# Attention decode with a gated FFN, forward and backward: the FFN's work cut into chains and put into another order

## The chip, the cores and the metric

The kernel runs on one core of a Trainium2 chip. The metric is the time of one execution on the device in microseconds. A core has five engines with a queue each: PE (TensorE, matrix products), DVE (VectorE), ACT (ScalarE), POOL (GpSimd) and SP (SyncE); in this kernel SP starts the loads and POOL the stores. Every engine takes its instructions in the order in which the build has put them.

## The reference, cut to what matters

One token attends to a cache of 4096 keys and values in 32 heads of 128, and beside it runs a gated FFN of width 1376. Wanted are the output and the gradients of x, of both caches and of all weights.

```python
xn  = layernorm(x)                                  # 1 x 512
q   = xn @ wq                                       # 32 heads x 128
p   = softmax((q @ k.T) * 128**-0.5)                # 1 x 4096 in each head
out = x + (p @ v) @ wo + (gelu(xn @ w_gate) * (xn @ w_up)) @ w_down
# and the gradients of sum(out * grad_out): dx, dk, dv, dwq, dwo, dw_gate, dw_up, dw_down
```

For one token dv of a head is the outer product of p and of the head's share of `grad_out @ wo.T`; dk is that of q and the gradient of the scores; every weight gradient is an outer product too. So large arrays are read once (K and V, 1 MB each in each head) and arrays as large are written once (dK and dV).

The FFN needs: g and u (the two products with xn), gelu and its derivative `dgl`, h = gelu(g)·u, `f = h @ w_down`, `dh = grad_out @ w_down.T`, then dg and du from dh (together `dgu`), dw_gate and dw_up as outer products of xn with dg and du, dw_down as that of h and grad_out, and the share of dx, `dg @ w_gate.T + du @ w_up.T`. The two products with a transposed weight need the weight blocks transposed on PE first.

## The kernel before, in words

Each head passes three stages, written as Python generators. `stage1(h)` (L133) loads K and V, 1 MB each, into a ring of six buffers (three heads), transposes each in 32 blocks of 128x128 on PE (L126), eight blocks to a PSUM tile, and copies each tile back: three on ScalarE (L130), the fourth on VectorE (L128). `stage2(h)` (L177) makes the scores in 32 narrow matmuls (L183), the softmax as a chain of small steps (L186 to L201: the maximum over partitions through a matmul with the identity, exp, the sum through a matmul with ones), dP with the transposed V (L205), and the gradient of the scores DS (L209 to L216). `stage3(h)` (L235) makes O (L247) and DQ (L266) from the untransposed V and K; these two free the buffers for a later head's load. It makes dV (L258) and dK (L272) on VectorE, 2.3 us each, and stores each by POOL (L263, L277); dV and dK share two buffers, so dV of a head waits until dV of the head before has been written. For every four heads dwo (L282) and dwq (L308) are stored.

Iteration h of the main loop (L573) lets `stage3(h)`, `stage2(h+1)` and `stage1(h+2)` take turns. The FFN is a further generator, `ffn_gen` (L319). Its first step, after iteration GATE_LOAD_H = 23, loads the three weights (4.2 MB) by POOL. To hold that load back, one element of each weight tile is first written by VectorE from `gate_t`, which head 23's O has filled. The later steps run after iterations 29, 30 and 31, nine at a time, and begin with `xn_g`, a copy of xn that is gated by head 29's O. What is left runs after the loop.

The order of the generators is not yet the order on the engines. The framework (Tile) schedules: it takes the program's order as a priority and its own estimate of when operands are ready, and puts each engine's instructions into one fixed queue. So an operation can stand far from where the code has it.

The FFN's steps before: the loads; g and u (L342, 88 narrow matmuls) and their roundings; gelu and its derivative (L354 to L384); f (L390, 44 matmuls) and dw_down (`dwd`, L397, in groups of four blocks, two buffers); eleven blocks of w_down transposed (L413), copied by ScalarE (L416) and multiplied with grad_out to dh (L421); dgu (L426 to L436); its transpose `tpr` (L439) and the broadcast of dg and du to all partitions (L450 on PE, L454 on ScalarE); the eight stores of dw_gate and dw_up (`dwt`, L459 and L460, two buffers); and eight times: transpose one 128-row strip of w_gate or w_up (L469, L473: 11 blocks), copy it by ScalarE (L470, L474), multiply it with dg or du (L478). After the loop the closing sums (L587 to L609) make the two small outputs.

PSUM: the narrow products, `gu_ps`, `f_ps`, `dh_ps`, `dx_ps`, the broadcasts and each head's scores (`SDP`) share three buffers of the tag `sdp`; all transposes share three of the tag `tp`.

Of the kernel before, what the change touches and what calls it, by code (L numbers as in the profile page):

```python
# [31 lines left out]
GATE_H = 29  # L32
GATE_LOAD_H = 23
# [14 lines left out]
def kernel(  # L48
# [268 lines left out]
    def ffn_gen():  # L317
        fsb1 = ffn_pools["fsb1"]
        fsb3 = ffn_pools["fsb3"]  # L319
        if True:  # L320
# [3 lines left out]
            gate0 = gate_t[:, 1:2]  # L324
            for wt in (wg_sb[:, 0, 0:1], wu_sb[:, 0, 0:1], wd_sb[:, 0, 0:1]):
                nc.vector.tensor_scalar(out=wt, in0=ones_bf[:, 0:1], scalar1=gate0, scalar2=None, op0=ALU.bypass)
            nc.gpsimd.memset(wg_sb[:, :, F:FPAD], 0.0)
            nc.gpsimd.memset(wu_sb[:, :, F:FPAD], 0.0)
            nc.gpsimd.memset(wd_sb[96:128, FT - 1, :], 0.0)
            nc.gpsimd.dma_start(out=wg_sb[:, :, 0:F], in_=B_w_gate.rearrange("(c p) f -> p c f", p=P))  # L330
            nc.gpsimd.dma_start(out=wu_sb[:, :, 0:F], in_=B_w_up.rearrange("(c p) f -> p c f", p=P))
            nc.gpsimd.dma_start(out=wd_sb[:, 0:FT - 1, :], in_=B_w_down[0:(FT - 1) * P, :].rearrange("(ft p) j -> p ft j", p=P))
            nc.gpsimd.dma_start(out=wd_sb[0:96, FT - 1, :], in_=B_w_down[(FT - 1) * P:F, :])
# [3 lines left out]
            gu_ps = lps.tile([P, 512], FP32, tag="sdp")  # L337
            for which, w_sb in enumerate((wg_sb, wu_sb)):
                for ft in range(FT):
                    col = which * 16 + ft  # L340
                    for c in range(NC):
                        nc.tensor.matmul(gu_ps[:, col:col + 1], lhsT=w_sb[:, c, ft * P:(ft + 1) * P], rhs=xn_g[:, c:c + 1],  # L342
                                         start=(c == 0), stop=(c == NC - 1))
            g_bf = fsb1.tile([P, FT], BF16)
            u_bf = fsb1.tile([P, FT], BF16)
            nc.vector.tensor_copy(out=g_bf[:], in_=gu_ps[:, 0:FT])
            nc.vector.tensor_copy(out=u_bf[:], in_=gu_ps[:, 16:16 + FT])
            g = fsb1.tile([P, FT], FP32)
            u = fsb1.tile([P, FT], FP32)
            nc.vector.tensor_copy(out=g[:], in_=g_bf[:])  # L350
            nc.vector.tensor_copy(out=u[:], in_=u_bf[:])
            yield
            g2 = fsb1.tile([P, FT], FP32)
            nc.vector.tensor_tensor(out=g2[:], in0=g[:], in1=g[:], op=ALU.mult)  # L354
            poly = fsb1.tile([P, FT], FP32)
            nc.vector.tensor_scalar(out=poly[:], in0=g2[:], scalar1=GELU_A, scalar2=1.0, op0=ALU.mult, op1=ALU.add)
            inner = fsb1.tile([P, FT], FP32)
            nc.vector.tensor_tensor(out=inner[:], in0=poly[:], in1=g[:], op=ALU.mult)
            th = fsb1.tile([P, FT], FP32)
            nc.scalar.activation(out=th[:], in_=inner[:], func=ACT.Tanh, scale=GELU_C)  # L360
            cdf = fsb1.tile([P, FT], FP32)
            nc.vector.tensor_scalar(out=cdf[:], in0=th[:], scalar1=0.5, scalar2=0.5, op0=ALU.mult, op1=ALU.add)
            gelu = fsb1.tile([P, FT], FP32)
            nc.vector.tensor_tensor(out=gelu[:], in0=cdf[:], in1=g[:], op=ALU.mult)
            gelu_bf = fsb1.tile([P, FT], BF16)
            nc.vector.tensor_copy(out=gelu_bf[:], in_=gelu[:])
            gelu_r = fsb1.tile([P, FT], FP32)
            nc.vector.tensor_copy(out=gelu_r[:], in_=gelu_bf[:])
            h_f = fsb1.tile([P, FT], FP32)
            nc.vector.tensor_tensor(out=h_f[:], in0=gelu_r[:], in1=u[:], op=ALU.mult)  # L370
            h_bf = fsb1.tile([P, FT], BF16)
            nc.vector.tensor_copy(out=h_bf[:], in_=h_f[:])
            h_r = fsb1.tile([P, FT], FP32)
            nc.vector.tensor_copy(out=h_r[:], in_=h_bf[:])
            t2 = fsb1.tile([P, FT], FP32)
            nc.vector.tensor_tensor(out=t2[:], in0=th[:], in1=th[:], op=ALU.mult)
            omt2 = fsb1.tile([P, FT], FP32)
            nc.vector.tensor_scalar(out=omt2[:], in0=t2[:], scalar1=-0.5 * GELU_C, scalar2=0.5 * GELU_C, op0=ALU.mult, op1=ALU.add)
            poly3 = fsb1.tile([P, FT], FP32)
            nc.vector.tensor_scalar(out=poly3[:], in0=g2[:], scalar1=3.0 * GELU_A, scalar2=1.0, op0=ALU.mult, op1=ALU.add)  # L380
            dgl = fsb1.tile([P, FT], FP32)
            nc.vector.tensor_tensor(out=dgl[:], in0=omt2[:], in1=poly3[:], op=ALU.mult)
            nc.vector.tensor_tensor(out=dgl[:], in0=dgl[:], in1=g[:], op=ALU.mult)
            nc.vector.tensor_tensor(out=dgl[:], in0=dgl[:], in1=cdf[:], op=ALU.add)  # L384
            yield
            f_ps = lps.tile([P, 512], FP32, tag="sdp")
            for c in range(NC):
                for ft in range(FT):
                    fs = min(P, F - ft * P)
                    nc.tensor.matmul(f_ps[:, c:c + 1], lhsT=wd_sb[0:fs, ft, c * P:(c + 1) * P], rhs=h_bf[0:fs, ft:ft + 1],  # L390
                                     start=(ft == 0), stop=(ft == FT - 1))
            nc.vector.tensor_copy(out=ffn_col[:], in_=f_ps[:, 0:NC])
            for ft in range(FT):
                fs = min(P, F - ft * P)
                if ft % 4 == 0:
                    dwd4 = fsb3.tile([P, 4, D_MODEL], BF16, tag="dwd4")
                nc.vector.tensor_scalar(out=dwd4[0:fs, ft % 4, :], in0=dy_bcast[0:fs, :], scalar1=h_r[0:fs, ft:ft + 1], scalar2=None, op0=ALU.mult)  # L397
                if ft % 4 == 3:
                    nc.gpsimd.dma_start(out=out_8[(ft - 3) * P:(ft + 1) * P, :].rearrange("(e p) j -> p e j", p=P), in_=dwd4[:])
                elif ft == FT - 1:  # L400
                    n_full = ft % 4
                    f0 = (ft - ft % 4) * P
                    if n_full > 0:
                        nc.gpsimd.dma_start(out=out_8[f0:f0 + n_full * P, :].rearrange("(e p) j -> p e j", p=P), in_=dwd4[:, 0:n_full, :])
                    nc.gpsimd.dma_start(out=out_8[ft * P:F, :], in_=dwd4[0:fs, ft % 4, :])
            yield
            dh = fsb1.tile([P, FT], FP32)
            nc.vector.memset(dh[96:128, FT - 1:FT], 0.0)
            for ft in range(FT):
                fs = min(P, F - ft * P)  # L410
                tpd = lps_t.tile([P, 8 * P], BF16, tag="tp")
                for c in range(NC):
                    nc.tensor.transpose(out=tpd[:, c * P:c * P + fs], in_=wd_sb[0:fs, ft, c * P:(c + 1) * P], identity=ident_bf[0:fs, 0:fs])  # L413
                wdT = fsb3.tile([P, NC, P], BF16, tag="wdT")
                if fs == P:
# [224 lines left out]
```

## Time and profile before

| what | value |
|---|---|
| time, median of six runs | 496.13 us (492.22 to 499.04) |
| the profiled execution's own time | 498.88 us |
| its span, first to last instruction | 496.7 us |
| PE busy, weight loads busy | 387.3 us (78%), 359.5 us (72%) |
| VectorE busy | 319.8 us (64%) |
| ScalarE busy | 261.1 us (53%) |
| GpSimd busy | 59.0 us (12%) |
| moved by DMA | 164.73 MB, mean 332 GB/s |
| mean granted TensorE clock | 0.643 |

How to read it: the span is the profiled execution's, and what lies around it (2.2 us) is in its time but not in the trace. The second part of the page cuts the span into 40 slices of 12.4 us; each digit is a busy share in tenths, and a row under them gives the GB/s that the transfers moved. A timeline row has start, duration, engine, line, operation, the tile written and the tiles read; in square brackets the idle time of that engine before it and what ended it. L numbers are lines of the kernel before.

### The profile page before, as it was taken

The page shows a single profiled execution, that of the slowest core. Times are in us where ns is not written, and L with a number is a line of the kernel's source. Part 1 is how long each engine was busy: PE and PEld are TensorE (multiplying, and loading weights), DVE is VectorE, ACT ScalarE, POOL GpSimd, SP SyncE. Part 2 cuts the span into 40 slices and gives each one's busy share as a digit, 9 for nine tenths or more (in the row PEclk, how much of TensorE's full clock was granted, in tenths as well). Part 3 has the DMA queues.
Part 4 walks back from the last instruction along what each step waited for, and adds up shares of the span by engine and source line. Part 5 has one row for each costly group of instructions (what it writes and reads, how often), then busy time and mean ns, then how long its engine had stood idle before and what let it go on. Part 6 is the DMA issues. An engine that isn't in the chain of part 4 may idle for free.

```text
span 496.7 us, 16676 instructions
## 1 busy us (share of the span) xinstructions
PE 387.3 (78%) x7309; PEld 359.5 (72%) x7309; DVE 319.8 (64%) x1067; ACT 261.1 (53%) x414; POOL 59.0 (12%) x107
## 2 busy tenths in 40 slices
PE   3588838697779788987898878985998699775691
PEld 3578727687678777977888877984898598674591
DVE  3156863687577767777566746784775266788364
ACT  1367806375456554663556546573456466532571
POOL 0100001010011001101110001100130002012122
PEclk9968956578557855686556555595557555775555
DMA  7977999599999999999997999989899979966547
GB/s 285 389 286 255 357 381 377 189 343 335 392 337 370 337 385 369 370 379 343 361 350 307 316 368 351 382 317 384 317 381 384 420 285 347 402 243 252 189 158 269
DMA packets 44509, 164.73 MB, mean 332 GB/s; under 512 B 19666, under 2 KB 23764, under 8 KB 27540
## 3 DMA queue, kind: packets, MB, share of 16 engines
q1 hardware_dynamic: 30924, 79.70, 46.5%
q0 software_dynamic: 13504, 83.96, 41.8%
q8 instruction: 57, 0.93, 0.7%
q14 instruction: 16, 0.13, 0.1%
q10 hardware_dynamic: 8, 0.00, 0.0%
HBM read 83.92 MB, written 79.73 MB: 329 GB/s over the span
## 4 chain that ended last, share of the span: by engine, by line
issue 63%; DMA 10%; PE 9%; POOL 8%; DVE 7%; ACT 1%; SPq 0%; POOLq 0%; ACTq 0%; DVEq 0%
PE tp L126 4%; DMA out_dram<-dK_sb 4%; POOL out_dram L263 3%; POOL out_dram L277 2%; DMA wo_1277<-in_A_wo_dram 2%; DMA K_sb<-in_A_k_cache_dram 2%; DVE dK_sb L272 2%; DVE dV_sb L258 1%; DMA out_dram<-dV_sb 1%; POOL out_dram L282 1%; POOL out_dram L308 1%; PE DQ_ps L266 1%; PE SDP L183 1%; DMA out_dram<-dwt 1%; DVE junkw L152 1%
## 5 line engine op out<-in xcount | busy, mean ns | idle before, releaser
L130 ACT COPY KT_sb<-tp 128x1024 bf16<-128x1024 bf16 x96 | 93.6, 1016 | 84.0 <-PE tp L126 77.2
L126 PE MATMUL tp<-ident_bf,K_sb 128*128 128x128 bf16 x1024 | 109.0, 282 | 18.8 <-DMA K_sb<-in_A_k_cache_dram 11.7
L126 PE MATMUL tp<-ident_bf,V_sb 128*128 128x128 bf16 x1024 | 108.6, 281 | 14.6 <-ACT VT_sb L130 8.7
L130 ACT COPY VT_sb<-tp 128x1024 bf16<-128x1024 bf16 x96 | 93.4, 1017 | 28.0 <-PE tp L126 25.3
L126 PEld LDWEIGHTS <-V_sb 128*128 128x128 bf16 x1024 | 91.4, 129 | 22.6 <-issue 20.6
L126 PEld LDWEIGHTS <-K_sb 128*128 128x128 bf16 x1024 | 90.4, 129 | 21.3 <-DMA K_sb<-in_A_k_cache_dram 12.7
L263 POOL DMA_DIRECT2D out_dram<-dV_sb x32 | 17.2, 538 | 216.7 <-DVE hilo L170 79.9
L266 PEld LDWEIGHTS <-K_sb 128*128 128x128 bf16 x1024 | 32.5, 103 | 12.4 <-issue 12.3
L183 PE MATMUL SDP<-Q_bf,KT_sb 128*128 128x1 bf16 x1024 | 38.2, 166 | 2.1 <-DVE hilo L170 1.8
L266 PE MATMUL DQ_ps<-DS_bf,K_sb 128*128 128x1 bf16 x1024 | 32.8, 166 | 8.3 <-DVE DS_bf L216 8.2
L183 PEld LDWEIGHTS <-KT_sb 128*128 128x128 bf16 x1024 | 36.3, 104 | 3.0 <-DVE KT_sb L128 1.9
L205 PEld LDWEIGHTS <-VT_sb 128*128 128x128 bf16 x1024 | 31.4, 102 | 7.8 <-issue 7.5
L162 ACT COPY wqTh<-tpw 128x512 bf16<-128x512 bf16 x32 | 18.9, 590 | 33.1 <-PE tpw L160 33.1
L205 PE MATMUL SDP<-DO_bf,VT_sb 128*128 128x1 bf16 x1024 | 32.2, 165 | 4.5 <-DVE tot L174 4.4
L247 PE MATMUL O_ps<-P_bf,V_sb 128*128 128x1 bf16 x1024 | 33.5, 166 | 0.7 <-DVE P_bf L201 0.7
L247 PEld LDWEIGHTS <-V_sb 128*128 128x128 bf16 x1024 | 32.9, 103 | 0.8 <-issue 0.7
L277 POOL DMA_DIRECT2D out_dram<-dK_sb x32 | 17.2, 539 | 131.4 <-DVE dxq_acc L290 26.8
L128 DVE COPY VT_sb<-tp 128x1024 bf16<-128x1024 bf16 x32 | 21.9, 685 | 10.7 <-PE tp L126 9.8
L128 DVE COPY KT_sb<-tp 128x1024 bf16<-128x1024 bf16 x32 | 21.9, 685 | 8.0 <-PE tp L126 7.3
L174 DVE TENSOR_SCALAR tot<-SDP 128x1 f32<-128x1 f32 x64 | 13.8, 218 | 20.0 <-PE SDP L172 19.8
L160 PE MATMUL tpw<-ident_bf,wqh 128*128 128x128 bf16 x128 | 18.1, 276 | 6.7 <-DVE KT_sb L128 6.0
L270 ACT ACTIVATE DSexp<-DS_f 128x64 bf16<-128x64 f32 x32 | 8.3, 260 | 23.4 <-DVE DS_f L213 23.4
(316 smaller groups left out, 604.8 us busy)
## 6 DMA issues: line engine op xcount, KB each, us to landing
K_sb<-in_A_k_cache_dram SPq DMA_DIRECT2D x32, 1024.0 KB, 8.3
V_sb<-in_A_v_cache_dram SPq DMA_DIRECT2D x32, 1024.0 KB, 9.5
out_dram<-dV_sb POOLq DMA_DIRECT2D x32, 1024.0 KB, 8.6
out_dram<-dK_sb POOLq DMA_DIRECT2D x32, 1024.0 KB, 8.2
wq_chunk<-in_A_wq_dram SPq DMA_DIRECT2D x4, 1024.0 KB, 7.3
wqh<-in_A_wq_dram SPq DMA_DIRECT2D x32, 128.0 KB, 10.9
out_dram<-dwo_sb POOLq DMA_DIRECT2D x8, 512.0 KB, 8.6
out_dram<-dwt POOLq DMA_DIRECT2D x8, 344.0 KB, 3.2
```

The costliest lines, as they stand in the source:

```text
L126: nc.tensor.transpose(out=tp[:, t8 * P:(t8 + 1) * P], in_=src[:, t, :], identity=ident_bf[:, :])
L128: nc.vector.tensor_copy(out=dstT[:, g4 * 8:(g4 + 1) * 8, :], in_=tp[:, :])
L130: nc.scalar.copy(out=dstT[:, g4 * 8:(g4 + 1) * 8, :], in_=tp[:, :])
L160: nc.tensor.transpose(out=tpw[:, c * P:(c + 1) * P], in_=wqh[:, c, :], identity=ident_bf[:, :])
L162: nc.scalar.copy(out=wqTh[:], in_=tpw[:, 0:NC * P].rearrange("p (c i) -> p c i", c=NC))
L174: nc.vector.tensor_scalar(out=tot[:], in0=SDP[:, c0:c0 + 1], scalar1=SDP[:, c0 + 1:c0 + 2], scalar2=None, op0=ALU.add)
L183: nc.tensor.matmul(SDP[:, C_S + t:C_S + t + 1], lhsT=KT_sb[:, t, :], rhs=Q_bf[:, h:h + 1], start=True, stop=True)
L205: nc.tensor.matmul(SDP[:, C_DP + t:C_DP + t + 1], lhsT=VT_sb[:, t, :], rhs=DO_bf[:, h:h + 1], start=True, stop=True)
L247: nc.tensor.matmul(O_ps[:, h:h + 1], lhsT=V_sb[:, t, :], rhs=P_bf[:, t:t + 1], start=(t == 0), stop=(t == T - 1))
L263: nc.gpsimd.dma_start(out=out_3[0, h].rearrange("(p t) d -> p t d", p=P), in_=dV_sb[:])
L266: nc.tensor.matmul(DQ_ps[:, h:h + 1], lhsT=K_sb[:, t, :], rhs=DS_bf[:, t:t + 1], start=(t == 0), stop=(t == T - 1))
L277: nc.gpsimd.dma_start(out=out_2[0, h].rearrange("(p t) d -> p t d", p=P), in_=dK_sb[:])
```

## The change: the FFN as interleaved chains

The FFN begins one head earlier (GATE_H 28, GATE_LOAD_H 22), and takes seven steps instead of nine after each iteration from there on. w_down is loaded ahead of the other two weights. The code of the FFN is moved into functions: `chainA(ft)`, one block of dh with its transposes; `chainB1` to `chainB3`, g and u, gelu, and f with dw_down; `chainC(c, which)`, the transposes of one strip of w_gate or w_up; `chainF(c, which)`, the product with that strip. They are called alternately. `dh` multiplies with `dy_g`, a copy of grad_out that is gated as `xn_g` is. The strips have a buffer each (eight instead of two in turn), since four are transposed before dgu is there. `dwd4` has one buffer instead of two. The stores of dw_gate and dw_up come after all strips.

```diff
-GATE_H = 29
-GATE_LOAD_H = 23
+GATE_H = 28
+GATE_LOAD_H = 22
...
+            nc.gpsimd.dma_start(out=wd_sb[:, 0:FT - 1, :], in_=B_w_down[0:(FT - 1) * P, :].rearrange("(ft p) j -> p ft j", p=P))
+            nc.gpsimd.dma_start(out=wd_sb[0:96, FT - 1, :], in_=B_w_down[(FT - 1) * P:F, :])
             nc.gpsimd.dma_start(out=wg_sb[:, :, 0:F], in_=B_w_gate.rearrange("(c p) f -> p c f", p=P))
             nc.gpsimd.dma_start(out=wu_sb[:, :, 0:F], in_=B_w_up.rearrange("(c p) f -> p c f", p=P))
-            nc.gpsimd.dma_start(out=wd_sb[:, 0:FT - 1, :], in_=B_w_down[0:(FT - 1) * P, :].rearrange("(ft p) j -> p ft j", p=P))
-            nc.gpsimd.dma_start(out=wd_sb[0:96, FT - 1, :], in_=B_w_down[(FT - 1) * P:F, :])
...
+            dy_g = fsb1.tile([P, NC], BF16)
+            nc.vector.tensor_scalar(out=dy_g[:], in0=dy_col_bf[:], scalar1=gate_t[:, 0:1], scalar2=None, op0=ALU.bypass)
...
-                    nc.tensor.matmul(dh_ps[0:fs, 0:1], lhsT=wdT[:, c, 0:fs], rhs=dy_col_bf[:, c:c + 1], start=(c == 0), stop=(c == NC - 1))
+                    nc.tensor.matmul(dh_ps[0:fs, 0:1], lhsT=wdT[:, c, 0:fs], rhs=dy_g[:, c:c + 1], start=(c == 0), stop=(c == NC - 1))
...
+            def chainC(c, which):
+                w_sb = wg_sb if which == 0 else wu_sb
+                wT = fsb1.tile([P, FT, P], BF16, tag=f"wT{c}{which}")
+                tpa = lps_t.tile([P, 8 * P], BF16, tag="tp")
+                for ft in range(8):
+                    nc.tensor.transpose(out=tpa[:, ft * P:(ft + 1) * P], in_=w_sb[:, c, ft * P:(ft + 1) * P], identity=ident_bf[:, :])
+                nc.scalar.copy(out=wT[:, 0:8, :], in_=tpa[:, :].rearrange("p (k i) -> p k i", k=8))
...
+                        dwd4 = fsb3.tile([P, 4, D_MODEL], BF16, tag="dwd4", bufs=1)
...
+            corder = [(c, w) for c in range(NC) for w in range(2)]
+            g, u = chainB1()
+            yield
+            chainA(0); chainA(1); yield
+            gelu_r, h_bf, h_r, dgl = chainB2(g, u)
+            yield
+            chainA(2); chainA(3); yield
+            chainC(*corder[0]); yield
+            chainA(4); chainA(5); yield
+            chainB3(h_bf, h_r); yield
+            chainC(*corder[1]); yield
+            chainA(6); chainA(7); yield
+            chainC(*corder[2]); yield
+            chainA(8); chainA(9); yield
+            chainC(*corder[3]); yield
+            chainA(10)
             dh_bf = fsb1.tile([P, FT], BF16)
...
+            def chainF(c, which):
+                wT = wTs[(c, which)]
+                dx_ps = lps.tile([P, 512], FP32, tag="sdp")
+                for ft in range(FT):
+                    col = which * FT + ft
+                    nc.tensor.matmul(dx_ps[:, 0:1], lhsT=wT[:, ft, :], rhs=dgu_bf[:, col:col + 1], start=(ft == 0), stop=(ft == FT - 1))
+                nc.vector.tensor_copy(out=dxn8[:, 2 * c + which:2 * c + which + 1], in_=dx_ps[:, 0:1])
...
+            for k in range(4):
+                chainF(*corder[k])
+            yield
...
+            for k in range(4, 8):
+                chainC(*corder[k])
+                chainF(*corder[k])
+                yield
+            nc.vector.tensor_reduce(out=dxn_ffn[:], in_=dxn8[:, :].rearrange("p (c w) -> p c w", w=2), axis=AXX, op=ALU.add)
             for which, (src_b, out_ap) in enumerate(((dg_bcast, out_6), (du_bcast, out_7))):
...
-            for _ in range(9):
+            for _ in range(7):
```

## The prediction

> **What bounds the kernel now.** I read the transfer rows first, then the timeline from 400 us on, then the transfers.
>
> ```profile
> DMA  7977999599999999999997999989899979966547
> GB/s 285 389 286 255 357 381 377 189 343 335 392 337 370 337 385 369 370 379 343 361 350 307 316 368 351 382 317 384 317 381 384 420 285 347 402 243 252 189 158 269
> ```
>
> For most of the span the 16 DMA engines are nine tenths busy or more; the change moves no byte out of it. From slice 36 on (435 us) 158 to 269 GB/s are left, so instruction chains set the end there. Busy time by stretch (columns: stretch and length, then busy us of PE, its weight loads, VectorE, ScalarE, GpSimd, then clock, DMA share, GB/s):
>
> ```profile
> 430.00:440.00 10.00, 8.95 (x139) 8.03 (x139) 7.30 (x20) 6.63 (x11) 0.74 (x2) 0.71 0.69 282
> 440.00:450.00 10.00, 6.50 (x234) 6.28 (x233) 8.72 (x39) 0.98 (x4) 1.39 (x3) 0.63 0.59 234
> 450.00:460.00 10.00, 5.09 (x103) 4.82 (x104) 8.51 (x29) 3.91 (x8) 2.64 (x4) 0.50 0.76 290
> 460.00:470.00 10.00, 7.50 (x88) 5.49 (x88) 3.88 (x17) 4.76 (x9) 2.35 (x4) 0.50 0.55 209
> 470.00:480.00 10.00, 9.10 (x204) 8.84 (x204) 5.09 (x27) 6.57 (x12) 1.98 (x4) 0.50 0.33 120
> ```
>
> VectorE carries 430 to 460; 460 to 480 is a chain through PE with VectorE half idle. The timeline's landmarks (start, us, engine, line):
>
> ```profile
> 428.33 0.34 PE L183 MATMUL SDP<-Q_bf,KT_sb 128*128 128x1 bf16 x8
> ...
> 445.90 2.29 DVE L272 TENSOR_TENSOR dK_sb<-b_8577,DSexp 128x4096 bf16<-128x4096 bf16 x1
> ...
> 456.39 2.27 DVE L272 TENSOR_TENSOR dK_sb<-b_8577,DSexp 128x4096 bf16<-128x4096 bf16 x1
> ...
> 463.12 0.28 PE L439 MATMUL tpr<-ident_bf,dgu_bf 128*22 128x128 bf16 x1 [1.85 <-DVE dgu_bf L435]
> ...
> 468.56 1.04 PE L183 MATMUL SDP<-Q_bf,KT_sb 128*128 128x1 bf16 x32
> ...
> 478.82 0.16 DVE L267 CAST DQ_bf<-DQ_ps 128x1 bf16<-128x1 f32 x1 [1.56 <-PE DQ_ps L266]
> ...
> 481.43 2.29 DVE L258 TENSOR_TENSOR dV_sb<-b_8588,Pexp 128x4096 bf16<-128x4096 bf16 x1
> ...
> 484.90 0.59 DVE L459 TENSOR_SCALAR dwt<-du_bcast,xn_colf 128x1408 bf16<-128x1408 bf16 x1 [0.69 <-DMA out_dram<-dwt]
> ```
>
> In order: head 30's scores end (428.7); head 29's dK (445.9); head 30's dK (456.4); the FFN gradient `dgu` reaches PE (463.1); head 31's scores (468.6); its DQ is copied out (478.8); its dV (481.4); the last `dwt` waits for its buffer (484.9). So head 30's softmax runs *beside* the K and V loads of head 31, and only head 31's stands in the open tail.
>
> **The change, step by step.** The arithmetic stays: the same transposes, matmuls and copies, plus one 128x4 gate copy (`dy_g`, 0.22 us by its twin at L336). What changes is the order, so I read the order in which the built kernel puts its instructions on each engine, and walked those queues, each in order, with the durations above.
>
> *Weights one head earlier.* wg, wu and wd (4.2 MB) go onto POOL's queue one head sooner. The transfers are saturated there (388 and 394 GB/s between 360 and 400 us), so this trades places: zero, bounds -3 to +3 us (0.69 to 1.02 DMA share in the rows from 400 to 440). It holds head 27's dV at about 421 us, as before (421.9): that waits for the write of head 26's dV.
>
> *Up to head 29's dK: +4.3 us.* On VectorE dV and dK of 27 now stand ahead of the last copy of V 29's transposes, and head 29's `negb` behind dV of 28. With 8.6 us as the median landing of a dV, dV 28 starts at 431.5, `negb` at 433.9; exp, VT 30's copy (0.68) and dK 28 follow to 437.6. Then P of 29 at 439 (its sum's matmul stands behind 16 wd and 11 wg transposes on PE), DS 443, dV 29 444.1 to 446.4. Ahead of dK 29 now stand the `dh` copies of chains A4 and A5, behind K 31's 29 transposes on PE (about 0.127 us each, L469's eight in 1.01): dK 29 starts at 450.2, not 445.9. Bounds: -4 (VectorE never waits) to +8 (both dV waits a full landing longer).
>
> *From there to `dgu`: +8.4 us; the step that decides.* Head 30's score matmuls, before at 428, now stand on PE behind the gate and up products, K 31's and most of V 31's transposes and the 44 f_ps matmuls. f_ps needs `h_bf`, on VectorE behind dK 29. So: dK 29 ends 452.5; GELU's 12 remaining small operations and KT 31's copy to 454.7; f_ps 1.3 to 456.1; then head 30's softmax in the open. Its price is head 31's now: 468.56 to 478.82, 10.3 us, hence 466.4. Behind it: chain C3's transposes with dh of A8 and A9 (2.3, to 468.7); three dwd (0.88); dV and dK of 30 (4.6), which need Pexp, on ScalarE now behind C1 to C3 and A10; the dgu chain (461.75 to 463.06, 1.3); `tpr` at 475.8 instead of 463.1, +12.7 with the step above. Bounds of this step: 0 (the softmax hidden) to +12 (dwd4 now has one buffer, so its two refills each wait a landing of 4.7 us; the softmax covers most of that).
>
> *From `dgu` to dV 31: 0 us.* Before, 463.1 to 481.4: 18.3. Now half of the C transposes are gone, but head 31 stands behind the rest. `tpr` 0.3; F0 to F3, 44 matmuls at 0.035, 1.5; scores 1.0; 22 broadcasts laced with 14 transposes 5.3 (463.3 to 468.6 before); dP 1.0; 9 transposes 1.15; O 1.1; F4 0.6; 8 transposes 1.0; DQ 1.1; F5 and three transposes 1.1; C7's eight 1.0; then C7's ScalarE copies 1.0 and 0.5, and Pexp behind them 0.3: 18. Bounds -4 (four C chains of 2.3 us less 5 us of F0 to F3 and waits) to +3.
>
> *From dV 31 to the end: +5.8 us.* Before: 481.43 to 496.7, 15.3. Now `dwt` of du, four of them in two buffers, comes last on VectorE and POOL, after dV 31, dK 31 and dwq, and the final sums stand behind it. The third dwt waits for the first one's write, behind three larger writes on POOL. Price: before, 3248 KB issued from 484.0 to 489.1 (dV, two dwt, dK, dwq) had landed by 494.5, 3.2 us per 1000 KB; now 2904 KB from dV's issue (2.55 after its start) land 9.4 later, at +12.0. dwt 0.6; the fourth 1.1 later (344 KB), at +13.7; the closing chain 489.24 to 496.7, 7.45: 21.1. Bounds +0.4 (no wait: 8.2 of VectorE work and 7.45) to +7.
>
> The Trainium skill speaks for such a change: "Perfetto Trace Analysis", Optimization Strategy, says that a kernel whose most-contended engine shifts may gain from interleaving its regimes. The rows at 450 to 480 look like that; by the rule alone the sum would be a gain, some of the 11 us that VectorE idles from 460 to 480. I go by the queue order: what is interleaved in front of head 30 is work it doesn't need.
>
> Its page "DMA: Bandwidth & Descriptors", Anatomy of one DMA, gives about 2.0 us plus bytes at 436 GB/s for one transfer: by that an estimate of 2.8 us for a dwt, and the last term would be 1.7 us smaller. The row of 3248 KB in 10.5 us already contains the queue, and I keep it.
>
> **Sum:** 4.3 + 8.4 + 0 + 5.8 = 18.5 us. The profiled execution took 498.88 us (span 496.7 and 2.2 around it), 2.75 over the median of 496.13; added to the median: 514.6 us. Within 1% (491.2 to 501.1) this kernel cannot be told from no change: its six runs spread over 1.4%.
>
> **Rivals.** *The interleaving closes VectorE's gaps.* The queue from dV 27 to dgu holds 8 dV or dK (18.3), 5 copies (3.4), 11 dwd (3.5), dwo and dwq (1.6) and 82 small ones at 0.1 (8.2): 35 us from 420.5, tpr at 455.6, 7.5 us early. Without the wait at the end that is 488.6, with it 494.4. For: 11 idle us between 460 and 480. Against: head 30's softmax is a chain of single results, with nothing large on VectorE's queue between its steps. It decides when the scores of 30 start before 441, i.e. 15 us sooner than I have them. Chance 0.14, half of it faster by over 1%.
>
> *Only the tail wait is real.* Head 30's softmax is covered (K 31 and V 31 come early enough, its load now being freed ahead of V 30's transposes), and 4.3 + 5.8 or the 5.8 alone stays: 502 to 506. Chance 0.14.
>
> *The gate brings nothing, head and FFN merely trade places:* 496, within 1%. For: no work is removed. Against: the two terms that lengthen the chain. Chance 0.06.
>
> *The single dwd4 buffer and the crossed queues hold up more than the softmax covers:* +12 for +8.4 and 2 more before: 520 to 525. Chance 0.16. My forecast (507 to 520): 0.50.
>
> **Numbers.** Faster by over 1% 0.07; within 1% 0.13 (the other half of the first, and the third); slower 0.80. From 496 to 523 leaves out the first rival (0.14) and the end of the fourth (0.04): it holds about 0.8.
>
> **What would show it.** dV 28 near 432, dK 29 near 450; head 30's 32 score matmuls after f_ps, near 456; `tpr` near 476; dV 31 18 us behind it; an idle VectorE ahead of the third du `dwt`, released by a DMA, of some 4 us; the end 21 us after dV 31's start. I am wrong if the scores of 30 come before 445, if dV 27 starts more than 5 us away from 421, or if the third dwt doesn't wait.

## The result, and the profile after

| | before | after |
|---|---|---|
| time, median | 495.65 us (16 runs, 491.54 to 499.04) | 504.51 us (8 runs, 499.92 to 510.37) |
| the profiled execution's own time | 498.88 us | 504.14 us |
| its span | 496.7 us | 502.2 us |
| mean granted TensorE clock | 0.643 | 0.640 |

The change makes the kernel slower: the ratio is 1.0171, 95% interval 1.0126 to 1.0216, that is +8.9 us (the interval is 6.2 to 10.7 us of 495.65). The forecast was 514.6 us, +18.5; its direction holds, its size is twice what was measured. Ratios, here and below, leave out disturbed runs (over 1.5% above the fastest of their kernel) and medians don't, so that where the runs scatter the two can point different ways; five of the profiles below are of such runs, so that only what lies behind a landmark (dV 22, explained below) is compared.

The second part of the page of the changed kernel, the transfers over 40 slices of 12.6 us:

```profile
DMA  7987999599999999999999999999999999452555
GB/s 281 391 293 293 300 412 401 211 322 350 341 371 381 316 387 344 367 362 373 334 395 368 385 323 391 330 369 340 394 416 394 345 354 363 190 210 85 214 204 217
```

The transfers are as full as before up to 427 us (the end of slice 34), and then drop to half and less, 8 us and one slice earlier than before (435 us). One slice moves 85 GB/s. So the open tail, in which instruction chains set the time, has become longer: 75 us instead of 62.

Stretches of 10 us of the changed kernel, with the columns of the same view before:

```profile
430.00:440.00 10.00, 8.92 (x235) 8.83 (x235) 6.67 (x32) 4.98 (x10) 1.17 (x2) 0.50 0.39 153
440.00:450.00 10.00, 7.32 (x143) 6.62 (x142) 6.33 (x26) 4.38 (x8) 1.30 (x2) 0.67 0.61 240
450.00:460.00 10.00, 9.11 (x176) 8.75 (x174) 5.76 (x31) 7.40 (x14) 0.76 (x1) 0.50 0.24 80
460.00:470.00 10.00, 4.24 (x92) 3.51 (x92) 7.02 (x19) 1.29 (x5) 2.35 (x4) 0.50 0.63 247
470.00:480.00 10.00, 9.90 (x173) 8.43 (x173) 4.28 (x22) 7.01 (x13) 2.72 (x4) 0.50 0.28 98
```

From 450 to 460 VectorE fell from 8.51 busy us to 5.76 and PE rose from 5.09 to 9.11: the FFN's transposes now stand there, and the large dV and dK products, which feed the stores, don't. They come later, from 460 to 470 (7.02 against 3.88), and from 470 to 480 VectorE is no busier than before (4.28 against 5.09). Over the five stretches it has 30.1 busy us instead of 33.5: the gaps moved and grew.

The timeline's landmarks of the changed kernel, with `f_ps`, head 30's DQ and dV, and the last store:

```profile
441.49 2.29 DVE L272 TENSOR_TENSOR dK_sb<-b_8577,DSexp 128x4096 bf16<-128x4096 bf16 x1
...
445.73 1.35 PE L430 MATMUL f_ps<-h_bf,wd_sb 128*128 128x1 bf16 x44
446.95 0.99 PE L183 MATMUL SDP<-Q_bf,KT_sb 128*128 128x1 bf16 x32
...
457.14 0.16 DVE L267 CAST DQ_bf<-DQ_ps 128x1 bf16<-128x1 f32 x1 [0.83 <-PE DQ_ps L266]
...
460.59 2.29 DVE L258 TENSOR_TENSOR dV_sb<-b_8588,Pexp 128x4096 bf16<-128x4096 bf16 x1 [0.51 <-ACT Pexp L256]
...
462.87 2.28 DVE L272 TENSOR_TENSOR dK_sb<-b_8577,DSexp 128x4096 bf16<-128x4096 bf16 x1
...
466.24 0.28 PE L487 MATMUL tpr<-ident_bf,dgu_bf 128*22 128x128 bf16 x1 [5.30 <-DVE dgu_bf L473]
...
467.75 0.99 PE L183 MATMUL SDP<-Q_bf,KT_sb 128*128 128x1 bf16 x32
...
482.79 2.29 DVE L258 TENSOR_TENSOR dV_sb<-b_8588,Pexp 128x4096 bf16<-128x4096 bf16 x1
...
495.21 0.59 DVE L515 TENSOR_SCALAR dwt<-du_bcast,xn_colf 128x1408 bf16<-128x1408 bf16 x1 [5.81 <-DMA out_dram<-dwt]
496.07 0.59 DVE L515 TENSOR_SCALAR dwt<-du_bcast,xn_colf 128x1408 bf16<-128x1408 bf16 x1 [0.27 <-DMA out_dram<-dwt]
...
499.93 0.29 SPq L645 DMA_DIRECT2D out_dram<-fin_rows  x1
```

Head 30's 32 score matmuls start at 446.95, behind `f_ps`, where before they ended at 428.7. Its DQ is copied out 9.2 us after the scores' end (457.14 against 447.94), a softmax in the open. The third du `dwt` waits 5.81 us for its buffer. All three were forecast, the scores for 456 us.

**How the stretches are counted.** The instructions stand in the same order in both kernels up to about head 22, and yet head 22's dV starts between 326.2 and 340.7 us in the profiles of this study, and differs between two profiles of one kernel (336.9 and 332.0 before, 332.1 and 328.4 after). This scatter has nothing to do with the change, so times below count from the start of head 22's dV (called dV 22), and each kernel's row has the stretches from there:

| from dV 22, us | forecast | before, two profiles | after, two profiles |
|---|---|---|---|
| to dV 27 | 84.1 | 85.0 and 84.1 | 80.7 and 77.9 |
| dV 27 to dK 29 | 29.2 | 24.0 and 25.7 | 28.7 and 29.4 |
| dK 29 to `tpr` | 25.6 | 17.2 and 17.2 | 24.8 and 24.4 |
| `tpr` to dV 31 | 18.3 | 18.3 and 18.3 | 16.6 and 16.6 |
| dV 31 to the end | 21.1 | 15.3 and 15.3 | 19.4 and 19.4 |
| all | 178.3 | 159.9 and 160.6 | 170.1 and 167.6 |

The forecast's column is made of its own times (dV 27 at 421, dK 29 at 450.2, `tpr` at 475.8, then 18.3 and 21.1; dV 22 of its profile at 336.9). The means of the bottom row differ by 8.6 us, the medians of the times by 8.9, so the loss lies behind dV 22; ahead of it the two profiles of the changed kernel happen to be 4.2 us shorter on the mean.

### The profile page after: what moved, and what is told of

Same layout as the page of the kernel before. It is cut to its first block, busy times and chain, and to the rows that moved or that the text cites. A ratio compares the mean times of both kernels' runs of the same rounds, so it can differ in the third digit from the quotient of the medians.

```text
span 502.2 us, 16676 instructions
## 1 busy us (share of the span) xinstructions
PE 387.1 (77%) x7309; PEld 359.2 (72%) x7309; DVE 322.2 (64%) x1068; ACT 262.0 (52%) x414; POOL 59.6 (12%) x107
## 4 chain that ended last, share of the span: by engine, by line
issue 62%; PE 12%; DMA 10%; POOL 9%; DVE 5%; ACT 2%; SPq 0%; POOLq 0%; DVEq 0%; ACTq 0%
PE tp L126 5%; POOL out_dram L277 3%; POOL out_dram L263 3%; DMA out_dram<-dK_sb 2%; DMA K_sb<-in_A_k_cache_dram 2%; DMA out_dram<-dV_sb 2%; DMA wo_1277<-in_A_wo_dram 2%; DVE dK_sb L272 2%; POOL out_dram L282 1%; DMA out_dram<-dwt 1%; POOL out_dram L308 1%; PE SDP L205 1%; PE DQ_ps L266 1%; PE tpa L364 1%; PE SDP L183 1%
## 5 line engine op out<-in xcount | busy, mean ns | idle before, releaser
L126 PE MATMUL tp<-ident_bf,V_sb 128*128 128x128 bf16 x1024 | 108.9, 281 | 18.3 <-ACT VT_sb L130 9.2
L266 PEld LDWEIGHTS <-K_sb 128*128 128x128 bf16 x1024 | 32.5, 103 | 10.3 <-issue 10.3
L277 POOL DMA_DIRECT2D out_dram<-dK_sb x32 | 17.2, 537 | 135.1 <-DVE dxq_acc L290 34.7
L172 PEld LDWEIGHTS <-ones_bf 128*128 128x128 bf16 x64 | 7.2, 117 | 15.8 <-DVE hilo L171 8.2
```

The lines of the kernel that those rows point to most:

```text
L126: nc.tensor.transpose(out=tp[:, t8 * P:(t8 + 1) * P], in_=src[:, t, :], identity=ident_bf[:, :])
L266: nc.tensor.matmul(DQ_ps[:, h:h + 1], lhsT=K_sb[:, t, :], rhs=DS_bf[:, t:t + 1], start=(t == 0), stop=(t == T - 1))
L277: nc.gpsimd.dma_start(out=out_2[0, h].rearrange("(p t) d -> p t d", p=P), in_=dK_sb[:])
```

## The experiments

The theory, from the forecast and the two traces: the loss is an exposed softmax of head 30 between `f_ps` and `dgu`, and a `dwt` that waits for its buffer at the end; the weights' earlier load is neutral. Against it: the load itself moves the stretch ahead of dV 27; the FFN's pieces in front of `dgu`, not the softmax, are the price of the middle; the gate at head 28 alone is. Ratios are to the kernel before on the same chip. Where a buffer count or a loop changes, the scheduler lays the queues anew, so each of these runs tests an order and not a single wait.

### The two kernels again

> The changed kernel as it is, beside the next three on one chip. 504 to 505 us again, and from the start of dV 22 to the end 170 us (170.1 in its first profile, 159.8 in that of the kernel before); if the two differ by more than 2 us, single profiles can't carry the stretches.

> The kernel before, unchanged, for a second profile of its stretches. Reading of the first one: dV 27 starts 85.0 us after dV 22, dK 29 109.0 after it, then 17.2 us to `tpr`, 18.3 to dV 31, 15.3 to the end. If the weights' step is what brings dV 27 forward in the changed kernel (80.7 and 77.9 there), dV 27 is again at 84 to 86 here. If that was chance of one profile, it is at 79 to 82. The three later stretches should repeat within 0.5 us.

Measured: the changed kernel 504.52 us, ratio 1.0142 (1.0064 to 1.0219); the kernel before, in its second profile, as in the table. From dV 22 to the end the changed kernel's two profiles differ by 2.5 us, more than the 2 that the expectation allowed for single profiles. But the difference lies ahead of dK 29: the stretches from there on repeat within 0.4 us, the one ahead of dV 27 within 2.8 only. What the table says of the tail is therefore no chance of one profile; what it says of dV 27 is known to some 3 us only.

### The weights' load alone

The kernel before, loading one head earlier:

```diff
-GATE_LOAD_H = 23
+GATE_LOAD_H = 22
```

> The kernel before with one edit: the FFN's weights are loaded after head 22 instead of 23. The FFN itself stays serial and starts after head 29. Theory A, the earlier load removes a hole in the transfers (0.53 DMA share from 400 to 405 us of the profile before): 3 to 5 us faster than before, 491 to 492 us, and the stores of dV 25 to 27 come 4 to 5 us earlier when counted from the store of dV 22. Theory B, my first step, which priced it at zero: 495 to 496 us, dV 27 71 us after dV 22 as in the profile before.

The changed kernel, loading one head later:

```diff
-GATE_LOAD_H = 22
+GATE_LOAD_H = 23
```

> The changed kernel with one edit: the weights are loaded after head 23, as before; the chains still start after head 28. Theory A: it loses what the earlier load gave, 508 to 509 us, dV 27's store 71 us after that of dV 22 instead of 67.6. Theory B, the load's place is worth nothing and the earlier dV 27 came from the reordered queues or from chance: 504 to 505 us.

Measured: the earlier load in the kernel before gives 1.0026 (0.9945 to 1.0107); dV 27 at 81.3 us after dV 22, the end at 161.9. The later load in the changed kernel gives 1.0082 (1.0006 to 1.0159), dV 27 at 84.1 and dK 29 at 113.6, close to the forecast's 84.1 and 113.3, but dK 29 to `tpr` takes 17.2 us and not 24.8 or 24.4, and the end is at 166.8.

So with the load at head 22, dV 27 comes earlier, and that buys nothing at the end: in the kernel before, `f_ps` is at 118.6 instead of 116.2 or 116.9. In the timeline the order there has turned round: dV 27 and dK 27 stand ahead of V 29's last copy (423.91), which before was done first (420.14). Here is the kernel before with the earlier load:

```profile
418.58 2.29 DVE L258 TENSOR_TENSOR dV_sb<-b,Pexp 128x4096 bf16<-128x4096 bf16 x1 [3.50 <-DMA out_dram<-dV_sb]
421.70 2.29 DVE L272 TENSOR_TENSOR dK_sb<-b,DSexp 128x4096 bf16<-128x4096 bf16 x1
423.91 0.68 DVE L128 COPY VT_sb<-tp 128x1024 bf16<-128x1024 bf16 x1
```

Over all profiles of this study dV 27 starts 75.7 to 82.6 us after dV 22 in the ten that load at 22, and 80.6 to 86.3 in the seven that load at 23 (means 79.9 and 83.5). The step is real on average, 3.6 us, and hardly larger than the scatter. Two heads earlier it is clearer: dV 25 starts 54.6 to 58.2 us after dV 22 with the load at 22 and 57.2 to 63.9 with the load at 23 (means 56.4 and 61.1).

The transfers show where it comes from. The 10 us that begin 60 us after dV 22, in the kernel before and in the changed one (columns as above):

```profile
396.88:406.88 10.00, 9.53 (x161) 9.12 (x161) 6.84 (x18) 5.36 (x8) 0.53 (x1) 0.50 0.75 274
392.15:402.15 10.00, 7.02 (x153) 6.74 (x152) 6.86 (x19) 5.04 (x6) 1.30 (x2) 0.67 0.95 346
```

With the load at 23 the transfers have a hole there, with the load at 22 it is filled (217 to 283 GB/s in six of the seven profiles with the load at 23; 321 to 369 in the seventh, whose dV 25 is the earliest of the seven, and in the ten with the load at 22). This is theory A of the first expectation, as far as dV goes, but without its gain in time.

In the changed kernel with the later load it is again the order that turns round. There `h_bf`, which `f_ps` needs, stands ahead of dK 29 on VectorE:

```profile
446.16 0.17 DVE L410 CAST h_bf<-h_f 128x11 bf16<-128x11 f32 x1
...
448.57 2.28 DVE L272 TENSOR_TENSOR dK_sb<-b,DSexp 128x4096 bf16<-128x4096 bf16 x1
```

So `f_ps` doesn't wait for dK 29; the scores of 30 end 113.5 us after dV 22 (115.8 and 113.3 with the earlier load), although dV 27 is later, and `tpr` follows them after 17.3 us (18.3).

### Head 30's scores earlier

Two FFN steps instead of seven after iteration 28, twelve after the later ones, so that the scores of 30 stand ahead of `f_ps` again:

```diff
-            for _ in range(7):
+            for _ in range(2 if h == GATE_H else 12):
```

> The changed kernel with one edit: after head 28 only two FFN steps are taken (g and u, chains A0 and A1), and twelve after head 29 and each later one. On PE this puts head 30's scores ahead of f_ps and of V 31's transposes; the queues up to V 30 and from the dgu transpose to the end stay as they were. If the exposed softmax of head 30 is the price of the middle stretch (dK 29's start to the dgu transpose 24.7 us, 17.2 before), that stretch falls to 17 to 20 us and the time to 498 to 501 us. If VectorE's and PE's work in that stretch is the bound whatever its order, the FFN's results come later by as much: 503 to 506 us.

Measured: 1.0148 (1.0057 to 1.024). The scores of 30 end 104.0 us after dV 22 instead of 115.8 and 113.3, ten us earlier, and `tpr` follows at 129.9 instead of 134.1 and 131.6: 2.9 us earlier on the mean. dK 29 to `tpr` is 22.6, not the 17 to 20 of an exposed softmax as the price. So ten us of earlier scores are worth 3 us here, not 8 or 10. The end comes at 164.1: two du `dwt` now stand ahead of dK 31, and the third waits 1.62 us instead of 5.81. What fills the softmax's place is seen on ScalarE, in the timeline of this run:

```profile
455.15 1.01 ACT L365 COPY wT<-tpa 128x1024 bf16<-128x1024 bf16 x1
456.05 0.49 ACT L369 COPY wT<-tpb 128x384 bf16<-128x384 bf16 x1
456.42 0.50 ACT L351 COPY wdT<-tpd 128x384 bf16<-128x384 bf16 x1
456.79 0.28 ACT L256 ACTIVATE Pexp<-P_f 128x64 bf16<-128x64 f32 x1
```

Head 30's `P_f` is ready at 446.4 there, but its `Pexp` stands in ScalarE's queue behind the chains' copies, until 456.79. dV 30 waits for it, and `dgu` stands behind dV 30 and dK 30 on VectorE.

### The strips behind `dgu`

That points at the four strips put in front of `dgu`. Here all eight are transposed behind it, as before, and the rest of the change stays:

```diff
-            chainC(*corder[0]); yield
...
-            chainC(*corder[3]); yield
...
-            for k in range(4):
-                chainF(*corder[k])
...
-            for k in range(4, 8):
+            for k in range(8):
                 chainC(*corder[k])
```

> The changed kernel, but all eight strips of w_gate and w_up are transposed behind `dgu`, as before. Theory A, the exposed softmax of head 30 is the price of the middle stretch: the scores of 30 still end about 114 us after dV 22, `tpr` follows 18 us later as now, dK 29 to `tpr` stays at 24 to 25 us, and the four strips cost 3 to 5 us more behind `tpr`; ratio 1.02 to 1.03. Theory B, what is put in front of `dgu` on PE and ScalarE is the price as much (four strips: ScalarE copies of 1.0 and 0.5 us each, three of them between 450 and 461): dK 29 to `tpr` falls by 3 to 5 us to 20 to 22, the stretch behind it grows by about as much; ratio 1.012 to 1.018.

> The changed kernel with all strips behind `dgu`, once more. Its first profile ended 163.7 us after dV 22 (the changed kernel: 170.1 and 167.6), with 20.4 us from dK 29 to `tpr`, 21.1 to dV 31 and 14.3 to the end, and no wait of a `dwt` for its buffer. If those 5 us are real, the ratio to the kernel before is 1.005 to 1.012. If the time of its first call holds: 1.018 to 1.03, and the loss lies ahead of dV 22, where the order is that of the changed kernel.

Measured: 1.0255 (1.0123 to 1.0387) with 4 runs, and 1.0086 (1.004 to 1.0131) with 12 on another chip; the second is the one to go by, and the two stand side by side. Its timeline:

```profile
441.40 0.94 PE L183 MATMUL SDP<-Q_bf,KT_sb 128*128 128x1 bf16 x32
...
455.34 0.28 PE L483 MATMUL tpr<-ident_bf,dgu_bf 128*22 128x128 bf16 x1
```

The softmax of 30 is as exposed as in the changed kernel (its scores end 113.7 us after dV 22, behind `f_ps`), and yet `tpr` comes 13.0 us after them, not 18.3. dK 29 to `tpr` is 20.4 in both profiles, in the range of the expectation for which the strips are the price. ScalarE shows how: head 30's `P_f` is done at 446.00 there, and at 452.08 in the changed kernel; its `Pexp`, in this run and in the changed kernel:

```profile
447.47 0.26 ACT L256 ACTIVATE Pexp<-P_f 128x64 bf16<-128x64 f32 x1
460.28 0.28 ACT L256 ACTIVATE Pexp<-P_f 128x64 bf16<-128x64 f32 x1
```

It starts 1.5 us after `P_f` without the strips, and 8.2 us after it behind them. Behind `tpr` the stretch to dV 31 grows to 21.1, as expected there, too. What neither expectation had: the end comes 14.3 us after dV 31, not 19.4. The scheduler now puts three of the four du `dwt` ahead of dV 31, and none waits for its buffer. From dV 22 to the end it is 163.7 and 162.2, some 6 us under the changed kernel; the better timed ratio, 1.0086 against 1.0171 and 1.0142, puts the gain at 3 to 4 us.

### Four buffers for `dwt`

To make room for two more, the last four strips use the buffers of the first four:

```diff
-                wT = fsb1.tile([P, FT, P], BF16, tag=f"wT{c}{which}")
+                wT = fsb1.tile([P, FT, P], BF16, tag=f"wT{(2 * c + which) % 4}")
...
-                    dwt = fsb3.tile([P, FPAD], BF16, tag="dwt")
+                    dwt = fsb3.tile([P, FPAD], BF16, tag="dwt", bufs=4)
```

> The changed kernel with four buffers for dwt instead of two (the room is made by letting strips 4 to 7 of the transposed weights take the four buffers of strips 0 to 3). VectorE then has no wait of 5.8 us ahead of the third du dwt. If that wait is what the end costs, 6 us faster than the changed kernel: 498 to 499 us. If the writes behind it end the kernel instead (2904 KB had landed 9.8 us after dV 31's store began, the last two dwt need 0.9 us each), only 2 to 3 us are gained: 501.5 to 502.5 us, and the last rows show a wait for a dwt or dwq write.

The same together with the earlier scores of 30:

> The changed kernel with both edits tried alone: two FFN steps after head 28 and twelve later, and four dwt buffers. If the late scores of head 30 and the wait at the end are separate costs, their gains add up: 10 us less than the changed kernel in the stretch from dV 22 to the end (6.0 and 4.7 alone), 494 to 496 us. If they are the same slack seen twice, 498 to 499 us, as each alone.

Measured: 1.0134 (1.0037 to 1.023), and 1.0128 (1.0063 to 1.0194) with both. With four buffers no `dwt` waits, and the end comes 14.3 us after dV 31 instead of 19.4; from dV 22 it is 165.4. Three du `dwt` stand ahead of dV 31 here as well, the timeline shows the second and third of them and what follows:

```profile
486.82 0.58 DVE L515 TENSOR_SCALAR dwt<-du_bcast,xn_colf 128x1408 bf16<-128x1408 bf16 x1
489.43 0.56 DVE L515 TENSOR_SCALAR dwt<-du_bcast,xn_colf 128x1408 bf16<-128x1408 bf16 x1
490.43 2.29 DVE L258 TENSOR_TENSOR dV_sb<-b,Pexp 128x4096 bf16<-128x4096 bf16 x1
```

The stretch of the wait is worth 5 us in the trace, on the mean of the two profiles 3.5 of it at the end; in the times this can't be told from the changed kernel (1.0171 and 1.0142). With both edits 164.6 us: the two gains do not add up. In part they are the same: the earlier scores alone had already taken the wait from 5.81 to 1.62 us. For the rest no run here tells why.

### The gate one head later

The chains stay, the gate goes back to head 29, and nine steps are taken:

```diff
-GATE_H = 28
+GATE_H = 29
...
-            for _ in range(7):
+            for _ in range(9):
```

> The changed kernel with the FFN begun after head 29, nine steps each time, as before; the chains, the weights' earlier load and dwt's two buffers stay. On PE head 30's scores then stand ahead of V 30's last transposes, and head 31's ahead of the last dh chains. If the late scores of head 30 are the main cost, the stretch from dK 29 to the dgu transpose falls from 24.7 to 17 to 19 us, and since head 31's softmax is now hidden too, the time falls to 490 to 496 us. If the chains themselves are the cost (more small operations interleaved on VectorE and ScalarE), it stays at 500 to 505 us.

The same with four `dwt` buffers, and then with the load at head 23 as well:

> The same with four dwt buffers (strips 4 to 7 again in the buffers of strips 0 to 3). Here all eight dwt come last on POOL, so with two buffers each pair waits for a write. If these waits bound the end, 3 to 6 us under the kernel with two buffers, 485 to 492 us; if the writes' own throughput ends the kernel (2752 KB of dwt at 3.2 us per 1000 KB), 0 to 2 us under it.

> The chains with both the gate and the weights' load at the heads of the kernel before (29 and 23) and four `dwt` buffers: the kernel with gate 29 and four buffers (ratio 1.000), the weights loaded one head later. If the earlier load costs some 2 us net, as between the kernels with load 22 and 23 so far: 0.994 to 0.998, dV 27 at 84 us after dV 22 instead of 75.7, and dK 29 no later than 105. If it costs nothing: 0.999 to 1.003.

Measured: gate 29 alone 1.0142 (1.0082 to 1.0201); with four buffers 1.0002 (0.9945 to 1.0059); with the later load 1.0139 (0.9918 to 1.0359), which tells nothing, its median being 493.8 us beside 495.19. With the gate at 29 both last heads' softmaxes are early, and dV 31 starts ahead of `tpr` (128.2 against 133.3 us after dV 22). dK 29 to `tpr` is 27.3 us, not the 17 to 19 expected, since head 31's work now stands in it. The end still comes at 165.8, because all eight `dwt` stand last, in two buffers. The timeline of VectorE shows it for the four of du:

```profile
494.93 0.58 DVE L515 TENSOR_SCALAR dwt<-du_bcast,xn_colf 128x1408 bf16<-128x1408 bf16 x1 [2.26 <-DMA out_dram<-dwt]
495.96 0.58 DVE L515 TENSOR_SCALAR dwt<-du_bcast,xn_colf 128x1408 bf16<-128x1408 bf16 x1 [0.45 <-DMA out_dram<-dwt]
499.05 0.59 DVE L515 TENSOR_SCALAR dwt<-du_bcast,xn_colf 128x1408 bf16<-128x1408 bf16 x1 [2.50 <-DMA out_dram<-dwt]
500.28 0.58 DVE L515 TENSOR_SCALAR dwt<-du_bcast,xn_colf 128x1408 bf16<-128x1408 bf16 x1 [0.64 <-DMA out_dram<-dwt]
```

The stores go in pairs, and each pair waits for the pair before: 2.3 and 2.5 us here, and 2.5 for the last two of dg. With four buffers it is 157.5 us from dV 22, with the later load as well 160.3, dV 27 at 86.3 and dK 29 at 113.5 (expected: 84, and 105 at the latest). By the times, 1.0002, the chains are thus not slower as such: with the gate at 29 and buffers enough, they take the time of the kernel before; with four buffers and the gate at 28 the ratio is 1.0134. By the trace the one with four buffers is helped by the earliest dV 27 of all (75.7); from dV 27 to the end it takes 81.8 us, that with the later load 74.0, and the kernel before 74.9 and 76.5.

### The kernel before, with head 31 ahead of `dgu`

If the order of the last head and the FFN counts, it can be had without the chains. In the kernel before, four steps instead of nine after iteration 29 put head 31's scores between the products for dh:

```diff
-            for _ in range(9):
+            for _ in range(4 if h == GATE_H else 14):
```

> The kernel before with four FFN steps instead of nine after iteration 29 and fourteen after the later ones, so that head 31's scores stand between the products for dh on PE, ahead of `dgu`, and not behind it. If an exposed softmax of the last head is what bounds the tail: dV 31 comes 5 to 8 us earlier (137 to 140 us after dV 22 instead of 144.6), `tpr` 5 to 9 us later, and the eight strips end the kernel; ratio 0.985 to 0.998. If head and FFN merely trade places, as a rival of the forecast had it: 0.998 to 1.006.

> The kernel before with four FFN steps after iteration 29 and fourteen after the later ones, once more. Its first profile ended 156.6 us after dV 22 (before: 159.8 and 160.6). If that is the order's doing: 156 to 158 again and a ratio of 0.990 to 0.996. If it was chance of one profile: 159 to 161 and a ratio within 0.997 to 1.003.

And with four `dwt` buffers:

> The same with four `dwt` buffers instead of two. If the third du `dwt`'s wait for its buffer (3.73 us in the profile with two) sets the end there, as it did in the changed kernel: the wait is gone, 152 to 154 us from dV 22 to the end, ratio 0.982 to 0.990. If the strips on PE and ScalarE set it, the wait was covered: 155.5 to 157, the ratio that of the kernel with two buffers.

Measured: 1.0008 (0.9913 to 1.0103) and 0.9898 (0.9782 to 1.0014); with four buffers 0.9934 (0.988 to 0.9988). dV 31 starts 124.3 and 125.2 us after dV 22 instead of 144.6 and 145.3, far more than the 5 to 8 us expected, and `tpr` comes at 124.6 and 125.5, not later than before (126.2 and 127.0) but earlier; the end comes at 156.6 and 157.5 instead of 159.9 and 160.6. From dV 31 to the end it is 32.4 us twice, and 28.9 with four buffers. The third du `dwt` with two buffers, from the timeline:

```profile
476.80 0.59 DVE L459 TENSOR_SCALAR dwt<-du_bcast,xn_colf 128x1408 bf16<-128x1408 bf16 x1 [3.73 <-DMA out_dram<-dwt]
```

With four there is no such wait (and dK 31 stands behind the `dwt` in the queue, not ahead of them). The stretch is 3.5 us shorter for a wait of 3.73, as it would be with the wait on the path; but dK 31's place has changed with it, so this isn't shown. From dV 22 this kernel ends at 156.7, in the range expected for a wait that was covered, and no earlier than the two with two buffers; the stretch up to dK 29 was 2.7 and 3.6 us longer in that profile, and how much of that is scatter is open. By its times it is the only kernel here whose interval lies under the one before, by 0.1 to 1.2%; whether the buffers or the order bring it can't be told by the times alone.

## Why the prediction was right in direction and wrong in size

By its own steps, from the table of stretches (overshoot: forecast less measured, the two profiles after):

- **"Weights one head earlier": zero, "It holds head 27's dV at about 421 us".** This is the step that failed. dV 27 came 3.4 and 6.2 us ahead of the forecast's 84.1 us, beyond the bound of -3, and this is the largest part of an overshoot of 8.2 and 10.7. The reason given, "The transfers are saturated there", rested on 360 to 400 us and on rows of 10 us from 400 on. From 400 to 405 us of the same profile the DMA share is 0.53, with 205 GB/s: a hole, and in the changed kernel the transfers are full at that place (0.75 and 0.95 of DMA share in the rows above). The landmark that was to show the forecast wrong, dV 27 more than 5 us away from 421, did so: 412.8 (of the 9.1 us to the 421.9 of before, 4.8 lie ahead of dV 22, 332.1 against 336.9). In the kernel before and in the changed one:

```profile
421.88 2.29 DVE L258 TENSOR_TENSOR dV_sb<-b_7390,Pexp 128x4096 bf16<-128x4096 bf16 x1 [0.74 <-DMA out_dram<-dV_sb]
...
412.80 2.29 DVE L258 TENSOR_TENSOR dV_sb<-b_7391,Pexp 128x4096 bf16<-128x4096 bf16 x1 [2.77 <-DMA out_dram<-dV_sb]
```

  It waits for the write of dV 26 in both, as the forecast said; that write landed earlier. With the load back at 23, dV 27 is at the forecast's 84.1 again. How much of the 3.4 and 6.2 is the load and how much is scatter stays open. So does what it was worth at the end: by the sum it is the largest part of the overshoot, but with the later load the changed kernel ended no later (166.8), because `f_ps` no longer stood behind dK 29.
- **"Up to head 29's dK": +4.3.** From dV 27 on, the walk through the queues gave 29.2 us, and 28.7 and 29.4 were measured: right. Since dV 27 came early, dK 29 ended up +0.3 and -2.5 against the profiles of before (109.3 less 109.0, 107.3 less 109.8).
- **"From there to dgu": +8.4, the step that decides.** 25.6 us forecast, 24.8 and 24.4 measured, +7.6 and +7.2: right in size, as long as `f_ps` stands behind dK 29 (17.2 in the run where it doesn't). The softmax was priced at 10.3 and took 10.2 (446.95 to 457.14). The step's cause was only half right. Of the 18.3 us from the scores of 30 to `tpr`, 5.3 are the strips in front of `dgu` (13.0 without them, with the softmax still in the open). Moving the scores ten us ahead brought 2.9, because `Pexp` stayed behind the chains' copies. The sum had priced the strips at "chain C3's transposes with dh of A8 and A9 (2.3)" and the softmax at 10.3.
- **"From dgu to dV 31": 0.** The stretch fell by 1.7 us, from 18.3 to 16.6: a term mis-sized, inside its bounds.
- **"From dV 31 to the end": +5.8.** +4.1, a term mis-sized by 1.7. The wait itself was forecast well: third `dwt` at +12.0 forecast, +12.42 measured (495.21 less 482.79), fourth at +13.7 and +13.28. What was too long is the closing chain, taken as 7.45 us from before. There the last instruction waited for the write of dwq, 1.8 us by the row below (view of SP's waits, kernel before: what waited, for what, us in total, times, longest). In the changed kernel the store of dwq is issued at 488.70, 11.2 us ahead of the last store, and the chain takes 5.44 us (502.2 less 496.76). The sum thus had 2.0 us too much there, and the fourth `dwt` came 0.4 early; against it, the sum had left out the fourth `dwt`'s own 0.7.

```profile
SPq L635 <- DMA out_dram<-dwq_10386: 1.8, 1, 1.8
```

Sum of the overshoots: 3.4 + 0.5 + 0.8 + 1.7 + 1.7 = 8.1 us of 8.2 for the first profile, 6.2 - 0.2 + 1.2 + 1.7 + 1.7 = 10.6 of 10.7 for the second.

Of the rivals, "only the tail wait is real" names the time that was measured (502 to 506), by sums that did not happen: it has the softmax covered, and the scores of 30 stood behind `f_ps`. That the interleaving closes VectorE's gaps fell with those scores: they were to start before 441 (104.1 us after dV 22 of its profile) and started at 446.95 (114.8). That head and FFN trade places is not true of this kernel, but nearly of the one with gate 29 and four buffers. The single `dwd4` buffer held nothing up that the profile shows: its copies run from 453.19 and 459.22 without a wait for a DMA.

The Trainium skill, "Perfetto Trace Analysis", Optimization Strategy, says that interleaving regimes whose most-contended engine differs may improve a kernel. The changed kernel is a case in which it did not: VectorE worked 30.1 us from 430 to 480 instead of 33.5, and the ratio is 1.0171. The kernel with head 31 moved ahead of `dgu` and four buffers, 0.9934, agrees with it if the order and not the buffers brought that, which isn't shown.

The skill's "DMA: Bandwidth & Descriptors", Anatomy of one DMA, would make a `dwt` of 344 KB an estimated 2.8 us. In the changed kernel 9.83 us passed from the issue of dV 31's store (485.38) to the third `dwt`, for the 2904 KB queued in between; the forecast's row gave 9.4. For the last two `dwt`, with nothing large ahead of them, the trace has 2.7 and 2.9 us, which agrees with the page; for a transfer behind others the row holds, and the page's figure is too small.

## What to carry to other kernels

Work that is moved forward into another chain's queue costs its copies as well as its matmuls: on an engine with one queue in fixed order, four strips that nobody needed yet delayed one small `Pexp`, and with it two large products and their stores. When a step is said to trade places because the transfers are full, read their rows finely enough to see a hole of 5 us, and carry the landmark that it moves through the rest of the sum instead of holding it. And look at the last stores of a kernel for their buffers: with two buffers of a small tile VectorE waited 3.73 us at the end of the kernel with head 31 ahead of `dgu` and 5.81 in the changed one, and not at all where three of the four stood ahead of dV 31 (the strips behind `dgu`).

## What had not been expected of the hardware

The body of the kernel, with instructions in the same order, varies by up to 14 us over the 17 profiles, which are of several chips (dV 22 between 326.2 and 340.7), while in the four kernels with two profiles each the stretches behind dK 29, where the transfers are not full, repeat within 0.4 us. Here the part with full transfers is where a profile says little about single microseconds.

From the issue of a store to its landing a `dwt` took 4.5 us as the median of the eight in the changed kernel's page, but the first du `dwt` was issued at 489.69 and held its buffer until 495.21, 5.5 us, behind three larger writes of its queue.
